# Query features of pair 0 held unturned, and the order around them

## The chip, the cores and the metric

The kernel runs on 1 core of one Trainium2 chip. The time is device microseconds from start to end of one execution. PE is TensorE's matmuls, PEld its weight loads, DVE VectorE, ACT ScalarE, POOL GpSimd, SP SyncE (here it only issues DMAs). "SPq" and "POOLq" are the queues of DMA issues of SP and POOL.

## The reference

A linear attention with sketched quadratic features, then a router that sends each token to one of 8 experts. q, k, v are (4, 4, 1088, 32): batch B, heads H, sequence S, head dimension D. S1 and S2 are (8, 32).

```python
def phi(x):
    a = np.einsum('rd,bhsd->bhsr', S1, x)
    b = np.einsum('rd,bhsd->bhsr', S2, x)
    return np.einsum('bhsi,bhsj->bhsij', a, b).reshape(*x.shape[:-1], r * r)
q_p, k_p = (phi(q), phi(k))                      # 64 features
kv = np.einsum('bhsf,bhsd->bhfd', k_p, v)
z = np.sum(k_p, axis=2)
out = einsum('bhsf,bhfd->bhsd', q_p, kv) / (einsum('bhsf,bhf->bhs', q_p, z)[..., None] + 1e-06)
x = out.transpose(0, 2, 1, 3).reshape(4352, 128)
logits = normed(x) @ normed(expert_emb).T / tau  # (4352, 8)
e = argmax(logits); gate = softmax(logits)[e]
y = gate * (relu(x @ w1[e]) @ w2[e])             # w1 (8, 128, 1024), w2 (8, 1024, 128)
```

## The kernel before

**Tiling.** The four batches are handled as two pairs, m = 0 and 1; the two batches of a pair lie on the two halves of the 128 partitions (u or i). The 1088 positions are 17 tiles (c) of 64 in each batch; GROUPS takes them as four groups of four tiles, the fourth with the single tile 16 (the "rest") beside it. So a group of one pair is 4 x 128 rows by 4 heads.

**Keys, for each group** (`keys`): `tr` turns the rows (L340, four PE transposes, copied to kT by ACT, L342); `ab` sketches them with S1 and S2 (L356; L353 for the rest); `b` copies the second sketch out of PSUM (L362, ACT); `prod` multiplies the two to 64 features (L367, DVE, out kp); `kv` accumulates kp against v and ones in one PSUM bank (L406). After the last group of a pair `total`, `tr_kv`, `kvT` and `kve` (L414 to L433) bring kv, z, and kv times the normalised expert embeddings into kz, the right side of the outputs. So an output matmul gives numerator, denominator and router logits at once.

**Queries, for each group** (`queries`): the same `tr`, `ab`, `b`, `prod` (out qp), then `tr_qp` turns the features (L478, eight transposes into a two-bank PSUM tile, copied by ACT, L481, to qpT), `nd` forms the outputs (L489, 32 matmuls into a two-bank tile), `x` divides and sums the logits (L498 to L505, DVE), `squares` gives the norms (L510 on ACT, L512 on POOL). The queries of pair 0 are ready before its keys are summed; their turned features wait in `held`, which is the second half of the tile of w2 (experts 4 to 7), so that these four experts' w2 are loaded late.

**Router, for each span** of 8 or 9 tiles (`router`): `best` and `pick` (L568 to L580) choose an expert; `place` (L588 to L595) counts on PE, with triangular and one matrices, where each token stands among those of its expert; `split` (L600 to L604), `mark` (L610) and `store` (L615, L616) prepare rows, and `write` (L620) sends them to HBM. Then `count` (L686, L687, out `full`) and `rest` of `plan_early` (L697 to L705), `find`, `digit`, `sums`, `tokens` of `table` (L662 to L679) make the list of tokens of each block of 128. The first 10 blocks (EARLY) come from pair 0 alone, the other 31 (LATE) from what remains of both pairs.

**Experts, for each of 41 blocks:** `fetch` (L736, gather by POOL), `turn` (L742, copied to xTb by DVE, L744), `weights` (L753 and L758 on DVE, L756 on ACT for the first ten: a copy of the chosen expert's w1 and w2 to a tile of its own), `up` (L767, relu L768), `share` (L775, L776), `down` (L782, L784) and the scatter to the output (L787).

**The order** is written out by hand. Each step is a closure put at (tick, rank); the lists are sorted by tick and rank and issued in that order under a manual schedule, so this is the program order of PE, DVE, ACT and POOL. Keys of pair 0 run in ticks 0 to 3 with the queries of pair 0 (K_AT, Q_AT); the outputs of pair 0 in ticks 4 to 7 with the keys of pair 1; the queries of pair 1 in ticks 8, 8, 9 and 10 and its outputs in ticks 8 to 11 (ND_AT); the experts start at tick 10. `put(after, rank, f)` puts f at its tick plus `after`. SP takes its DMAs in program order, and a DMA waits for a queue slot.

**PSUM.** ps_small has two banks (`t`), ps_big two tiles of two banks each (`big`), and `acc` and `ab` have one bank each. In ticks 0 to 3 the sketches of keys and queries of a group lie in the two halves of the one `ab` bank. `ps_big` serves `tr_qp`, `nd` and later `up`.

Of the kernel before, what the change touches and what calls it, by code (L numbers as in the profile page):

```python
# [11 lines left out]
F32 = mybir.dt.float32  # L12
# [7 lines left out]
P = 128  # L20
B, H, S, D = 4, 4, 1088, 32
R = 8
# [35 lines left out]
def kernel(  # L58
# [43 lines left out]
    def load_q(m, c0, c1):  # L102

        for i in range(2):
            r = slice(i * HALF, (i + 1) * HALF)
            at = q.offset + (2 * m + i) * H * S * D + c0 * D
            nc.sync.dma_start(q_sb[m][r, :, c0:c1].rearrange("p h c d -> p h (c d)"),
                              bass.AP(tensor=q.tensor, offset=at, ap=[[NC * D, HALF], [S * D, H], [1, (c1 - c0) * D]]))

# [59 lines left out]

    held = w2_sb[:, E // 2:].rearrange("p e f d -> p e (f d)").rearrange("p e (b n) -> p e b n", b=2)  # L170

# [55 lines left out]
    def iota(shape, pattern, base, mult, name):  # L227
        ti = work.tile(shape, I32, tag="iota", bufs=1, name=name + "_i")
        nc.gpsimd.iota(ti[:], pattern=pattern, base=base, channel_multiplier=mult)
        t = consts.tile(shape, F32, name=name)  # L230
        nc.vector.tensor_copy(t[:], ti[:])
        return t
# [30 lines left out]
    def iotas():  # L263
        li = work.tile([P, P], I32, tag="iota", bufs=1, name="lane_i")
        nc.gpsimd.iota(li[:], pattern=[[1, P]], base=0, channel_multiplier=0)
        nc.vector.tensor_copy(lane, li)
        part = iota([P, 1], [[1, 1]], 0, 1, "part")
        nc.vector.tensor_scalar(before, lane, part[:, 0:1], 1.0 / P, op0=ALU.is_gt, op1=ALU.mult)
        nc.vector.tensor_scalar_mul(lanes, bview(lane, [[1, P], [0, WIDE]]), 1.0 / P)

        nc.vector.tensor_scalar_mul(prefer, lane[:, :E], -1.0 / (2 * E))
        nc.vector.tensor_scalar_mul(base, lane[:, :E], float(KEYS))
        tok_i = work.tile([P, 3, NM * NCP], I32, tag="iota", bufs=1, name="tok_i")
# [69 lines left out]
    def tile_of(n, shape, tag):  # L345
        return work.tile(shape, F32, tag=tag if n > 1 else tag + "1", bufs=2 if n > 1 else 1, name=tag)
# [17 lines left out]

    def features(ab, b, n, tag):
        t = tile_of(n, [P, n, H, R * R], tag)
        nc.vector.tensor_mul(t.rearrange("p j h (i k) -> p (j h) i k", i=R),  # L367
                             ab[:, :, 0].unsqueeze(3).broadcast_to([P, n * H, R, R]),
                             b.unsqueeze(2).broadcast_to([P, n * H, R, R]))
        return t  # L370

    def ab_bank(tick, n):

        if (tick, n) not in ab_ps:
            ab_ps[tick, n] = ps_small()[:, :2 * P] if n == 1 else ps_one("ab")
        return ab_ps[tick, n]

    def keys(m, c0, c1, put):
# [6 lines left out]
        def ab():  # L385
            s["ab"] = sketch(ab_bank(put.tick, n)[:, n * HALF:], s["kT"], n)

# [39 lines left out]
        def kve():  # L427
# [3 lines left out]
            for u in range(2):  # L431
                r = slice(u * HALF, (u + 1) * HALF)
                nc.scalar.copy(kz[m][r, :, :, u, D + 1:], ps[r, :, :, u])  # L433
        put(-1, 52, tr)
        put(0, 50, ab)
        put(0, 51, b)
        put(0, 54, prod)

        first = c0 >= NC - 5 and m == 0
        put(1, 47 if first else 55, kv)  # L440
        if c1 == NC:
            put(1, 47.5 if first else 56, total)
            put(1, 48.5 if first else 60, tr_kv)
            put(1, 48.6 if first else 64, kvT)
            put(1, 53 if first else 82.5, kve)

    xg, ssq, lg, squared = {}, {}, {}, {}

    def queries(m, c0, c1, put, put_nd):
# [15 lines left out]
        def ab():  # L465
            s["ab"] = sketch(ab_bank(put.tick, n)[:, :n * HALF], s["qT"], n)

# [3 lines left out]
        def prod():  # L471
            s["qp"] = features(s["ab"], s["b"], n, "qp")

        def tr_qp():
            ps = ps_big() if n > 1 else ps_small().rearrange("p (b n) -> p b n", b=2)
            for j in range(n):
                for p in range(2):
                    nc.tensor.transpose(ps[:, p, j * P:(j + 1) * P],  # L478
                                        s["qp"][:, j, 2 * p:2 * p + 2].rearrange("p h f -> p (h f)"), ident)
            s["qpT"] = held[:, c0 // 4] if m == 0 and n > 1 else tile_of(n, [P, 2, w], "qpT")  # L480
            nc.scalar.copy(s["qpT"], ps[:, :, :w])  # L481

        def nd():
            ps = ps_big().rearrange("p b (u n) -> p (b u) n", u=2) if n > 1 else ps_small().unsqueeze(1)
            W = 2 * COLS
            for j in range(n):
                for i in range(2):
                    for p in range(2):
# [3 lines left out]
                            kz[m][:, i, p].rearrange("p h d -> p (h d)"), start=True, stop=True)  # L492
            s["hs"] = ps[:, :n, :2 * W].rearrange("p n (h d) -> p n h d", h=H)

        def x():
# [17 lines left out]
        last = c0 >= NC - 5  # L513
        if m == c0 == 0:

            for i, f in enumerate((tr, ab, b, prod)):
                put(0, (51.1, 51.2, 51.3, 54.1)[i], f)
        elif m == 0:
            put(-1, 53, tr)
            put(0, 49, ab)  # L520
            put(0, 50.5, b)
            put(0, 53, prod)
        else:

            behind = c0 == 4
            put(*((0, 53.5) if behind else (-1, 84 if c0 == 8 else 53)), tr)
            put(0, 83 if behind else 49, ab)
            put(0, 83.1 if behind else 50.5, b)
            put(0, 88 if behind else 53, prod)
        if m == 0:  # L530
            put(1, 48 if last else 57, tr_qp)
        else:
            put(*((0, 82) if c0 == 0 else (1, 20)), tr_qp)
        first = m == 1 and c0 == 0
        put_nd(0, 89 if first else 70, nd)
        put_nd(0, 90 if first else 71, x)
        put_nd(*((0, 77) if last else (1, 51.5)), squares)
        if c1 == s1:
            best, pick, place, split, mark, store, write = router(m, s0, s1, g)
            put_nd(0, 80, best)  # L540
            put_nd(0, 81, pick)
            put_nd(1, 64 if m == 0 and c1 == NC else 90, write)

            if c1 < NC:
                put_nd(1, 83, place)
                put_nd(1, 84, split)
                put_nd(1, 85, mark)
                put_nd(1, 86, store)
            elif m == 0:
                put_nd(1, 56, place)  # L550
                put_nd(1, 57, split)
                put_nd(1, 59, mark)
                put_nd(1, 63, store)
            else:
                put_nd(1, 56, place)
                put_nd(1, 57, split)
                put_nd(1, 86, mark)
                put_nd(1, 87, store)

    counts = []  # L560

    def router(m, c0, c1, g):
        n = c1 - c0
# [18 lines left out]
        def place():  # L582
# [3 lines left out]
            hot = oh[m, c0]  # L586
            ps = ps_small()[:, :n * E].rearrange("p (j e) -> p j e", e=E)
            nc.tensor.matmul(ps, before, hot, start=True, stop=False)  # L588
# [4 lines left out]
            counts.append(total[m, c0])  # L593
            s["t"] = work.tile([P, SPAN, E], F32, tag="lt", name="lt")[:, :n]
            nc.vector.tensor_mul(s["t"], ps, hot)  # L595

        def split():

            t0, t1 = m * NCP + c0, m * NCP + c1
            f = work.tile([P, SPAN], F32, tag="mx8", name="mx8")[:, :n]  # L600
            nc.vector.reduce_sum(out=f, in_=s["t"], axis=AX.X)
            nc.vector.tensor_scalar(place_k[:, t0:t1], f, WHOLE, -WHOLE, op0=ALU.add, op1=ALU.add)
# [79 lines left out]
    def tokens_by_expert(rounded, out):  # L682

        ps = ps_small()[:, :E]
        for i, t in enumerate([rounded] + counts):
# [114 lines left out]
    for i, group in enumerate(GROUPS):  # L800
        for tiles in group:
            for m in range(NM):
                keys(m, *tiles, put_at(K_AT[m][i]))
                queries(m, *tiles, put_at(Q_AT[m][i]), put_at(ND_AT[m][i]))
    put_at(0)(0, 90, more_constants)
    put_at(0)(0, 91, iotas)
    put_at(1)(0, 60, norm_emb)
    put_at(2)(0, 56, scale_emb)
    put_at(3)(0, 51, turn_emb)
    put_at(1)(0, 91, lambda: clear(0))  # L810
    put_at(2)(0, 91, lambda: clear(1))
    put_at(3)(0, 57, place_emb)
    put_at(ND_AT[0][-1])(0, 78, lambda: [load_w2(e) for e in range(E // 2, E)])

# [12 lines left out]
    assert first == Q_AT[1][-1]  # L827
    put_at(first)(-1, 73, lambda: turn(0))

# [3 lines left out]
    put = put_at(table1)  # L833
    put(0, 56.5, count)
    put(1, 40, rest)
# [10 lines left out]
    for i in range(NBLK + 1):  # L846
# [6 lines left out]
        if i + 1 < NBLK:  # L853
            put(0, 72, lambda i=i: turn(i + 1))
        if i < NBLK:
# [41 lines left out]
```

## Time and profile before

| what | value |
|---|---|
| median of 3 runs | 252.95 us (252.93 to 253.91) |
| the profiled execution | 255.82 us |
| its span | 253.87 us |
| PE, PEld busy | 223.2 us (88%), 214.1 us (84%) |
| DVE, ACT, POOL busy | 134.2, 118.1, 100.7 us |
| moved by DMA | 24.30 MB, mean 96 GB/s |

A line of the profile has the line number in the kernel, the engine and the operation, then out <- in by the names of tiles. Where a tile was named in a helper, all its users have that line: L340 turns keys and queries both, and L367 is the product of both, told apart by kp and qp. A tile in `held` shows as w_sb, the name of the weights' tile. Times in a timeline are from the span's start. A matmul's record overlaps the next, so for groups the distance of two starts says more than the duration.

Landmarks of the execution before, from its timeline (start, us): first key turn (L340) 6.14; first key and query sketches (L356) 7.47 and 9.84; next pairs of sketches 13.64, 18.80, 24.45; first turn of query features (L478) 17.77; first output (L489) 41.17; DVE full (L687) 61.12; first write of rows (L620) 54.28; the first fetch (L736) 70.03; first matmul of the expert blocks (L767) 77.96; blocks 3, 6 and 7 at 99.10, 112.74 and 116.50; last scatter (L787) 245.32.

### The profile page before, as it was taken

To read this page: it belongs to the slowest core of one execution; us is meant where nothing else is said; L and a number is where in the kernel's file an instruction comes from. 1 tells how busy PE (TensorE), PEld (TensorE's weight loads), DVE (VectorE), ACT (ScalarE), POOL (GpSimd) and SP (SyncE) were. 2 spreads that over 40 slices of the span, in tenths; PEclk is the share of its full clock that TensorE was granted. 3 is DMA by queue.
4 is the path that set the end of the run, shared out by engine and by line. 5 is a ranking of instruction groups with operands and counts; after the bars stand their busy time and mean duration, and the time that the engine had idled before them with its cause. 6 is when DMAs were issued, how large, how long until landed. Compare 5 with 4: busy or idle time off the path is not lost. (4 is left out here: it accounts for less than half of the span.)

```text
span 253.9 us, 6275 instructions
## 1 busy us (share of the span) xinstructions
PE 223.2 (88%) x2455; PEld 214.1 (84%) x2455; DVE 134.2 (53%) x399; ACT 118.1 (47%) x307; POOL 100.7 (40%) x115
## 2 busy tenths in 40 slices
PE   7679498986877989999999999999999999999930
PEld 6467397876766888999999999999999999999930
DVE  4285504899754788773454455455545544554300
ACT  2426225646552776656635444543444354345410
POOL 3001000312081335455654655565556556552330
PEclk9999869999795899999999999999999999999995
DMA  5969999939620021311111111101111111120000
GB/s 142 268 136 348 232 321 343 361 139 271 227 49 12 14 92 46 110 34 40 37 32 34 35 35 43 40 26 35 39 32 44 34 38 32 35 42 25 7 0 0
DMA packets 22174, 24.30 MB, mean 96 GB/s; under 512 B 5306, under 2 KB 18629, under 8 KB 22145
## 3 DMA queue, kind: packets, MB, share of 16 engines
q1 hardware_dynamic: 19520, 18.79, 25.2%
q0 software_dynamic: 2624, 5.11, 8.4%
q8 instruction: 19, 0.31, 0.5%
q14 instruction: 11, 0.08, 0.1%
HBM read 18.09 MB, written 6.26 MB: 96 GB/s over the span
## 5 line engine op out<-in xcount | busy, mean ns | idle before, releaser
L767 PE MATMUL ps_big<-xTb,wb 128*128 128x128 f32 x656 | 82.0, 279 | 3.1 <-DVE xTb L744 2.2
L767 PEld LDWEIGHTS ps_big<-xTb,wb 128*128 128x128 f32 x656 | 78.2, 195 | 3.7 <-DVE xTb L744 2.4
L787 POOL DMA_INDIRECT out_dram<-y,dst_i x41 | 46.6, 1137 | 59.3 <-ACT y L784 47.4
L768 ACT ACTIVATE hT<-ps_big 128x1024 f32<-128x1024 f32 x41 | 42.0, 1024 | 58.5 <-PE ps_big L767 45.3
L736 POOL DMA_INDIRECT xs<-rows,src_i x41 | 40.9, 998 | 21.7 <-DVE xg L500 9.8
L782 PE MATMUL ps_acc<-wb,hT 128*128 128x128 f32 x336 | 41.0, 275 | 0.0
L782 PEld LDWEIGHTS ps_acc<-wb,hT 128*128 128x128 f32 x336 | 39.2, 192 | 0.0
L782 PE MATMUL ps_ab<-wb,hT 128*128 128x128 f32 x320 | 39.0, 275 | 0.0
L782 PEld LDWEIGHTS ps_ab<-wb,hT 128*128 128x128 f32 x320 | 37.4, 192 | 0.0
L753 DVE COPY wb<-w_sb 128x1024 f32 x41 | 28.6, 698 | 13.8 <-issue 12.8
L512 POOL TENSOR_TENSOR xg<-ssq,half_c 128x4 f32<-128x4 f32 (+1 forms) x10 | 9.4, 942 | 46.9 <-ACT sq L510 42.1
L775 DVE TENSOR_SCALAR gate<-gate 128x1 f32<-128x1 f32 x41 | 6.2, 152 | 38.2 <-ACT hT L768 22.9
L758 DVE COPY wb<-w_sb 128x1024 f32 x31 | 21.3, 686 | 0.0
L744 DVE COPY xTb<-ps_t 128x128 f32<-128x128 f32 x41 | 11.9, 290 | 15.8 <-PE ps_t L742 12.7
L367 DVE TENSOR_TENSOR kp<-ps_ab,kb 128x1024 f32<-128x1024 f32 x8 | 9.7, 1211 | 15.0 <-ACT kb L362 9.8
L367 DVE TENSOR_TENSOR qp<-ps_ab,qb 128x1024 f32<-128x1024 f32 x8 | 9.8, 1220 | 9.3 <-ACT kb L362 5.0
L784 ACT ACTIVATE y<-ps_acc,gate 128x128 f32<-128x128 f32 x21 | 7.7, 368 | 12.4 <-PE ps_acc L782 11.9
L784 ACT ACTIVATE y<-ps_ab,gate 128x128 f32<-128x128 f32 x20 | 7.4, 368 | 11.3 <-PE ps_ab L782 10.3
L510 ACT ACTIVATE sq<-xg 128x128 f32<-128x128 f32 x34 | 10.5, 310 | 3.8 <-DVE xg L500 2.9
L742 PE MATMUL ps_t<-ident,xs 128*128 128x128 f32 x41 | 11.4, 278 | 1.0 <-ACT qT L342 0.8
L772 ACT ACTIVATE probs<-xs 128x8 f32<-128x8 f32 x41 | 11.9, 291 | 0.0
L756 ACT COPY wb<-w_sb 128x1024 f32 x10 | 10.4, 1047 | 1.8 <-DMA w_sb<-in_moe_w_dram 1.3
(178 smaller groups left out, 256.8 us busy)
## 6 DMA issues: line engine op xcount, KB each, us to landing
w_sb<-in_moe_w_dram SPq DMA_DIRECT2D x16, 512.0 KB, 8.4
k<-in_k_dram SPq DMA_DIRECT2D x4, 512.0 KB, 5.2
v<-in_v_dram SPq DMA_DIRECT2D x4, 512.0 KB, 7.0
rows<-xg SPq DMA_DIRECT2D x3, 616.5 KB, 3.9
rows<-xg SPq DMA_DIRECT2D x3, 548.0 KB, 2.8
q<-in_q_dram SPq DMA_DIRECT2D x2, 544.0 KB, 7.1
xs<-rows,src_i POOLq DMA_INDIRECT x41
out_dram<-y,dst_i POOLq DMA_INDIRECT x41
```

Source lines behind the costliest of these rows:

```text
L367: nc.vector.tensor_mul(t.rearrange("p j h (i k) -> p (j h) i k", i=R), ab[:, :, 0].unsqueeze(3).broadcast_to([P, n * H, R, R]), b.unsqueez ...
L736: nc.gpsimd.indirect_dma_start(out=xs[i][:], out_offset=None, in_=rows[t][:, :], in_offset=bass.IndirectOffsetOnAxis(ap=src_i[t][:, j:j + ...
L742: nc.tensor.transpose(ps[:, :P], xs[i][:, :DM], ident)
L744: nc.vector.tensor_copy(xT[i], ps[:, :P])
L753: nc.vector.tensor_copy(wb[i][:, 0], w1_sb[:, bass.ds(e, 1)].rearrange("p o f -> p (o f)"))
L758: nc.vector.tensor_copy(wb[i][:, 1], w2)
L767: nc.tensor.matmul(ps[:, u, j * P:(j + 1) * P], w[:, f * P:(f + 1) * P], x, start=True, stop=True)
L768: nc.scalar.activation(hT[i], ps, ACT.Relu)
L772: nc.scalar.activation(p, xs[i][:, DM:DM + E], ACT.Exp, scale=xs[i][:, ROW - 1:], accum_out=gate[i])
L782: nc.tensor.matmul(ps, h[:, f * P:(f + 1) * P], w[:, f], start=f == 0, stop=f == NF - 1)
L784: nc.scalar.activation(y, ps, ACT.Copy, scale=gate.pop(i)[:, 0:1])
L787: nc.gpsimd.indirect_dma_start(out=out[:, :], out_offset=bass.IndirectOffsetOnAxis(ap=dst_i[t][:, j:j + 1], axis=0), in_=y[:], in_offset=N ...
```

## The change

Three things are changed in what is done, and many ranks in the order of it.

- **Loads of q** go by head over all 128 partitions (four DMAs in place of two over 64 partitions each).
- **Pair 0's query features** are written by `prod` into `held` as they are. Their turn (`tr_qp`, now without its copy) and the copy (`qpT`, a step of its own) move from ticks 1 to 4 to pair 1's key ticks: group 0 to tick 4, the others to the tick before their outputs.
- **Banks.** In ticks 0 to 3 `ab_bank` gives the sketches a two-bank tile, one bank for queries and one for keys; from tick 4 on, the halves of `ab` as before. The router's counts go to the unused end of a bank of `nd`'s tile (`spare`) or, for the last span of a pair, to a `table_bank` that also takes the counts by expert. The product of counts and choice moves from `place` to `split`.
- **Order.** The constants and iotas (two buffers now) move from rank 90 of tick 0 to 45; `scale_emb` to rank 45 of tick 2; `turn_emb` and `place_emb` from tick 3 to tick 4; the four late w2 loads from rank 78 to 48 of tick 7, all behind the first write of rows; the second write of rows from rank 64 to 58 of tick 8, with its `store` ahead of the table; `turn(0)` to rank 21 of tick 10, `turn(i + 1)` from rank 72 to 45. In the expert part nothing else is changed.

```diff
     def load_q(m, c0, c1):
-        for i in range(2):
-            r = slice(i * HALF, (i + 1) * HALF)
-            at = q.offset + (2 * m + i) * H * S * D + c0 * D
-            nc.sync.dma_start(q_sb[m][r, :, c0:c1].rearrange("p h c d -> p h (c d)"),
-                              bass.AP(tensor=q.tensor, offset=at, ap=[[NC * D, HALF], [S * D, H], [1, (c1 - c0) * D]]))
+        for h in range(H):
+            nc.sync.dma_start(q_sb[m][:, h, c0:c1].rearrange("p c d -> p (c d)"),
+                              bass.AP(tensor=q.tensor, offset=q.offset + (2 * m * H + h) * S * D + c0 * D,
+                                      ap=[[H * S * D, 2], [NC * D, HALF], [1, (c1 - c0) * D]]))
...
-    def ab_bank(tick, n):
+    def ab_bank(tick, n, u):
         if (tick, n) not in ab_ps:
-            ab_ps[tick, n] = ps_small()[:, :2 * P] if n == 1 else ps_one("ab")
-        return ab_ps[tick, n]
+            ps = ps_small() if n == 1 else ps_big() if tick < n_g else ps_one("ab")
+            ab_ps[tick, n] = ps if n > 1 and tick < n_g else ps[:, :2 * n * HALF].rearrange("p (u n) -> p u n", u=2)
+        return ab_ps[tick, n][:, u, :n * HALF]
...
         def prod():
-            s["qp"] = features(s["ab"], s["b"], n, "qp")
+            t = held[:, c0 // 4].rearrange("p (j h f) -> p j h f", j=4, h=H) if m == 0 and n > 1 else None
+            s["qp"] = features(s["ab"], s["b"], n, "qp", t)
...
-            s["qpT"] = held[:, c0 // 4] if m == 0 and n > 1 else tile_of(n, [P, 2, w], "qpT")
-            nc.scalar.copy(s["qpT"], ps[:, :, :w])
+            s["ps"] = ps[:, :, :w]
+
+        def qpT():
+            s["qpT"] = tile_of(n, [P, 2, w], "qpT")
+            nc.scalar.copy(s["qpT"], s["ps"])
...
+        if m == 0:
+            put(*((0, 51.1) if c0 == 0 else (-1, 53)), tr)
+            put(0, 53.1 if c0 == 0 else 50, ab)
+            put(0, 53.2 if c0 == 0 else 50.5, b)
+            put(0, 54, prod)
+            for i, f in enumerate((tr_qp, qpT)):
+                put_nd(*((0, 47.7 + 0.02 * i) if c0 == 0 else (-1, 57)), f)
+            put_nd(0, 70, nd)
+            put_nd(0, 71.5 if n == 1 else 71, x)
...
-            ps = ps_small()[:, :n * E].rearrange("p (j e) -> p j e", e=E)
+            ps = s["ps"] = bank()[:, :n * E].rearrange("p (j e) -> p j e", e=E)
...
-            s["t"] = work.tile([P, SPAN, E], F32, tag="lt", name="lt")[:, :n]
-            nc.vector.tensor_mul(s["t"], ps, hot)
...
         def split():
+            t = work.tile([P, SPAN, E], F32, tag="lt", name="lt")[:, :n]
+            nc.vector.tensor_mul(t, s["ps"], oh[m, c0])
...
-    put_at(0)(0, 90, more_constants)
-    put_at(0)(0, 91, iotas)
+    put_at(0)(0, 45, more_constants)
+    put_at(0)(0, 46, iotas)
...
-    put_at(2)(0, 56, scale_emb)
-    put_at(3)(0, 51, turn_emb)
+    put_at(2)(0, 45, scale_emb)
+    put_at(4)(0, 47.75, turn_emb)
...
-    put_at(3)(0, 57, place_emb)
-    put_at(ND_AT[0][-1])(0, 78, lambda: [load_w2(e) for e in range(E // 2, E)])
+    put_at(4)(0, 47.9, place_emb)
+    put_at(ND_AT[0][-1])(0, 48, lambda: [load_w2(e) for e in range(E // 2, E)])
...
-    put_at(first)(-1, 73, lambda: turn(0))
+    put_at(first)(0, 21, lambda: turn(0))
...
-            put(0, 72, lambda i=i: turn(i + 1))
+            put(0, 45, lambda i=i: turn(i + 1))
```

More of the change, by code (lines that the diff above doesn't have):

```diff
@@ L168 @@
     w2_sb = consts.tile([P, E, NF, DM], F32, name="w2_sb")
-    held = w2_sb[:, E // 2:].rearrange("p e f d -> p e (f d)").rearrange("p e (b n) -> p e b n", b=2)
+    held = w2_sb[:, E // 2:].rearrange("p e f d -> p e (f d)")
     def load_w2(e):
@@ L227, in iota @@
     def iota(shape, pattern, base, mult, name):
-        ti = work.tile(shape, I32, tag="iota", bufs=1, name=name + "_i")
+        ti = work.tile(shape, I32, tag="iota", bufs=2, name=name + "_i")
         nc.gpsimd.iota(ti[:], pattern=pattern, base=base, channel_multiplier=mult)
@@ L263, in iotas @@
     def iotas():
-        li = work.tile([P, P], I32, tag="iota", bufs=1, name="lane_i")
+        li = work.tile([P, P], I32, tag="iota", bufs=2, name="lane_i")
         nc.gpsimd.iota(li[:], pattern=[[1, P]], base=0, channel_multiplier=0)
@@ L274, in iotas @@
         nc.vector.tensor_scalar_mul(base, lane[:, :E], float(KEYS))
-        tok_i = work.tile([P, 3, NM * NCP], I32, tag="iota", bufs=1, name="tok_i")
+        tok_i = work.tile([P, 3, NM * NCP], I32, tag="iota", bufs=2, name="tok_i")
         nc.gpsimd.iota(tok_i[:, 0].rearrange("p (m c) -> p m c", m=NM), pattern=[[-2 * S, NM], [-1, NCP]], base=NOWHERE,
@@ L363, in second, with features @@
         return b
-    def features(ab, b, n, tag):
-        t = tile_of(n, [P, n, H, R * R], tag)
+    def features(ab, b, n, tag, t=None):
+        if t is None:
+            t = tile_of(n, [P, n, H, R * R], tag)
         nc.vector.tensor_mul(t.rearrange("p j h (i k) -> p (j h) i k", i=R),
@@ L385, in ab @@
         def ab():
-            s["ab"] = sketch(ab_bank(put.tick, n)[:, n * HALF:], s["kT"], n)
+            s["ab"] = sketch(ab_bank(put.tick, n, 1), s["kT"], n)
         def b():
@@ L433, in kve @@
                 nc.scalar.copy(kz[m][r, :, :, u, D + 1:], ps[r, :, :, u])
[L434 to L437, printed above, removed]
+        put(-1, 49.5 if m == 0 and c0 == 4 else 52, tr)
+        ahead = m == 1 and c0 == 0
+        put(0, 47.8 if ahead else 49.8, ab)
+        put(0, 47.9 if ahead else 49.9, b)
+        put(0, 53, prod)
         first = c0 >= NC - 5 and m == 0
@@ L441, in keys @@
         if c1 == NC:
[L442 to L447, printed above, removed]
+            put(1, 47.5 if first else 55.2, total)
+            put(1, 47.705 if first else 55.6, tr_kv)
+            put(1, 47.71 if first else 57.9, kvT)
+            put(1, 53 if first else 58.5, kve)
+    xg, ssq, lg, spare = {}, {}, {}, {}
     def queries(m, c0, c1, put, put_nd):
@@ L465, in ab @@
         def ab():
-            s["ab"] = sketch(ab_bank(put.tick, n)[:, :n * HALF], s["qT"], n)
+            s["ab"] = sketch(ab_bank(put.tick, n, 0), s["qT"], n)
         def b():
@@ L493, in nd @@
             s["hs"] = ps[:, :n, :2 * W].rearrange("p n (h d) -> p n h d", h=H)
+            spare[m, c0] = ps[:, 0, 2 * W:]
         def x():
@@ L513, in queries @@
         last = c0 >= NC - 5
[L514 to L522, printed above, removed]
-        else:
[L525 to L537, printed above, removed]
+        step = c0 // 4
+        if m == 0:
[7 more added lines that the diff above has]
+            put_nd(0, 71.5 if n == 1 else 71, x)
+            put_nd(*((1, 55.3 if n == 1 else 53.6) if last else (1, 53.5)), squares)
+        else:
+            turn_at = ((-1, 53), (0, 53.5), (-1, 59), (-1, 53), (-1, 53))[step]
+            put(*turn_at, tr)
+            put(*((-1, 70.6), (0, 55.8), (0, 49), (0, 22), (0, 22))[step], ab)
+            put(*((-1, 70.7), (0, 58.7), (0, 50.5), (0, 22.1), (0, 22.1))[step], b)
+            put(*((-1, 71.2), (0, 88), (0, 53), (0, 53), (0, 53))[step], prod)
+            put(*((0, 55.5) if c0 == 0 else (1, 20)), tr_qp)
+            put(*((0, 58) if c0 == 0 else (1, 20)), qpT)
+            put_nd(0, 84 if c0 == 0 else 70, nd)
+            put_nd(0, 90 if c0 == 0 else 71, x)
+            put_nd(*((0, 77) if last else (1, 53.5)), squares)
@@ L538, in queries @@
         if c1 == s1:
-            best, pick, place, split, mark, store, write = router(m, s0, s1, g)
+            bank = (lambda: spare[m, c1]) if c1 < NC else (lambda: table_bank[m][:, 0])
+            best, pick, place, split, mark, store, write = router(m, s0, s1, g, bank)
             put_nd(0, 80, best)
             put_nd(0, 81, pick)
-            put_nd(1, 64 if m == 0 and c1 == NC else 90, write)
+            put_nd(1, 58 if m == 0 and c1 == NC else 90, write)
             if c1 < NC:
-                put_nd(1, 83, place)
+                put_nd(1, 70.5, place)
@@ L549, in queries @@
             elif m == 0:
+                put_nd(1, 55.9, lambda: table_bank.append(ps_big()))
                 put_nd(1, 56, place)
                 put_nd(1, 57, split)
+                put_nd(1, 57.2, store)
                 put_nd(1, 59, mark)
-                put_nd(1, 63, store)
             else:
-                put_nd(1, 56, place)
-                put_nd(1, 57, split)
+                put_nd(1, 75, lambda: table_bank.append(ps_big()))
+                put_nd(1, 75.1, place)
+                put_nd(1, 76, split)
                 put_nd(1, 86, mark)
@@ L560, with router @@
     counts = []
-    def router(m, c0, c1, g):
+    table_bank = []
+    def router(m, c0, c1, g, bank):
         n = c1 - c0
@@ L593, in place @@
             counts.append(total[m, c0])
-            s["t"] = work.tile([P, SPAN, E], F32, tag="lt", name="lt")[:, :n]
-            nc.vector.tensor_mul(s["t"], ps, hot)
         def split():
             t0, t1 = m * NCP + c0, m * NCP + c1
+            t = work.tile([P, SPAN, E], F32, tag="lt", name="lt")[:, :n]
+            nc.vector.tensor_mul(t, s["ps"], oh[m, c0])
             f = work.tile([P, SPAN], F32, tag="mx8", name="mx8")[:, :n]
-            nc.vector.reduce_sum(out=f, in_=s["t"], axis=AX.X)
+            nc.vector.reduce_sum(out=f, in_=t, axis=AX.X)
             nc.vector.tensor_scalar(place_k[:, t0:t1], f, WHOLE, -WHOLE, op0=ALU.add, op1=ALU.add)
@@ L682, in tokens_by_expert @@
     def tokens_by_expert(rounded, out):
-        ps = ps_small()[:, :E]
+        ps = table_bank[-1][:, 1, :E]
         for i, t in enumerate([rounded] + counts):
@@ L833 @@
     put = put_at(table1)
-    put(0, 56.5, count)
+    put(0, 75.5, count)
     put(1, 40, rest)
```

## The prediction

> **What bounds the kernel now.** I read the page's table by engine first, then the window table by stage, the waits of PE, the PE timeline of 24 to 42, and the DMA issues. PE is the busiest engine (88%). The chain of waits names only the last store, so the stages have to come from the window table. Its columns are the window and its length, then busy us and (x instructions) of PE, PE's weight loads, DVE, ACT and POOL, then granted clock, DMA share and GB/s.
>
> ```profile
> 6.00:38.00 32.00, 24.05 (x354) 20.84 (x355) 13.32 (x36) 11.55 (x29) 1.50 (x5) 0.89 1.01 260
> 38.00:60.00 22.00, 18.71 (x413) 16.87 (x412) 16.90 (x50) 12.81 (x54) 4.46 (x5) 1.00 0.85 278
> 60.00:78.00 18.00, 12.53 (x162) 10.85 (x157) 13.07 (x41) 9.03 (x22) 6.44 (x7) 0.88 0.48 153
> 78.00:95.00 17.00, 15.65 (x174) 14.54 (x175) 10.83 (x39) 10.23 (x36) 4.39 (x4) 0.83 0.12 44
> ...
> 120.00:140.00 20.00, 20.00 (x182) 20.00 (x181) 10.13 (x28) 9.77 (x22) 10.66 (x10) 1.00 0.14 35
> ```
>
> From 120 on PE is 100% busy at full clock: one expert block each 3.68 us (L767 twice in a row 112.74 to 116.50, then steady). The change touches nothing there, so what the expert blocks start earlier passes one to one to the end. Before it, no engine is full: 6 to 38 has 8 us of PE idle, 60 to 78 has 5.5, and the clock is under 1 in three windows. The waits say where (us in total, times, longest):
>
> ```profile
> PE ps_t L340 <- DVE en_blk L322: 3.5, 1, 3.5
> PE ps_big L767 <- DVE xTb L744: 2.2, 1, 2.2
> PE ps_ab L356 <- DVE qp L367: 1.8, 1, 1.8
> ```
>
> The first is in the timeline (start, us, engine, line; idle before in brackets); the turns behind it cost 1.98 and 1.97 where they cost 1.15 and 1.09 at 22.35 and 23.43. The window table on 3.41 us shows why:
>
> ```profile
> 26.16 0.28 PE L318 MATMUL ps_t<-ident,emb 8*128 8x8 f32 x2
> 29.98 1.09 PE L340 MATMUL ps_t<-ident,k 128*128 128x128 f32 x4 [3.53 <-DVE en_blk L322]
> 31.00 1.98 PE L406 MATMUL ps_acc<-v,kp 128*64 128x64 f32 x32
> 32.91 1.97 PE L478 MATMUL ps_big<-ident,qp 128*128 128x128 f32 x8
> ...
> 41.17 1.04 PE L489 MATMUL ps_big<-kz,w_sb 128*64 128x82 f32 x23 [0.92 <-ACT kz L433]
> ```
> ```profile
> 25.91:29.33 3.42, 0.54 (x10) 0.38 (x7) 2.62 (x4) 0.61 (x4) 0.00 (x0) 1.00 0.97 232
> 29.33:32.74 3.41, 2.76 (x36) 2.46 (x36) 0.59 (x4) 0.59 (x1) 0.00 (x0) 0.50 1.04 240
> 32.74:36.15 3.41, 3.41 (x40) 2.96 (x37) 0.00 (x0) 1.01 (x1) 0.00 (x0) 0.50 1.11 338
> ```
>
> An idle window gives half clock for two windows. It happens again after 63.46:66.87 (2.22 busy) and 73.70:77.11 (1.24 busy); the first expert block at 77.96 takes 3.78 to the next group, 1.95 at full clock.
>
> **Part 1, up to the first output (L489, now 41.17).** What goes: the 3.5 wait, since emb's turn and its placement leave tick 3 for tick 4; the half clock behind it, by starts 0.5 + 0.8 + 0.9 + 0.5 = 2.7; the 1.8 wait of the query sketch for the query product, since keys and queries no longer share a bank; two of pair 0's four turns L478 (0.86 each, 1.7) and the rest's 0.4, now behind the first output; and waits for two turned copies, 0.67 and 0.62. Sum 11.4. What comes: in ticks 0 to 3 both sides lie in one two-bank tile, so the first query sketch waits for the first key product (9.14 to 10.05: 0.9) and the next for the key copy (0.5). That gives 10.0. The constants and iotas now come ahead of the first products on DVE and POOL; DVE is idle until 10.0 in that stretch (0.00 busy in 6 to 10), which covers them; without that cover the first products start up to 1.3 later (one lanes row of 0.82 and smaller ones). A walk instruction by instruction through the order of the new program, with these rows, puts the first output at 30.5, a gain of 10.6. I take the walk; the 0.6 stays in the range. DVE now writes pair 0's query products into the space that held the turned ones, the same 1.21 each: nothing.
>
> **Query loads.** Two loads over 64 partitions become four over 128:
>
> ```profile
> q<-in_q_dram SPq DMA_DIRECT2D x2, 288.0 KB, 9.7
> q<-in_q_dram SPq DMA_DIRECT2D x2, 256.0 KB, 5.4
> ```
>
> While q is in flight the windows move 215 to 241 GB/s, with k and v 342 to 384. The new loads are nearest to k and v in shape (128 partitions), so I take their rate. SP issues two more for each of three loads, 0.6 each; the first 1.2 go ahead of k's second half (lands 13.6, wanted about 13.0 in the walk), which the faster half MB (0.9) nearly repays. Bounds: 0, and +2.5 if they run as q now does (q's second part lands at 16.0, wanted at 13.5).
> The Trainium skill, "DMA: Bandwidth & Descriptors", section Bandwidth, speaks against this part: it asks for 1 MiB or more in a transfer, and has 138 GB/s at 64 KB against 341 at 1 MB; the new loads have 128 to 144 KB. By it (an estimate) half a MB would take 3.8 us instead of the 2.4 that it takes at 215, so 1.4 later, and the total would be near 245.9. No row here has such small loads on the whole width.
>
> **Part 2, pair 1's key ticks, to the expert counts (DVE full L687, now 61.12).** Two turns and the rest's (2.0) and their ACT copies (1.01 each) come in. ACT has 9 us free of 22 there, so the copies are hidden; the turns are not, since DVE (16.90 of 22) and PE alternate. The walk from the first reciprocal to full is 21.9 where it is 18.5 now: 2.0 from the turns, 1.3 from products and outputs that wait on one another through two big banks. Bounds for the latter 0 to 2.6 (twice). Full comes at 53.7: gain 7.4.
> Here a rule of the Trainium skill speaks against the change: "TensorE: Matmul & The Clock Gate", Part 4 (PE-mode transpose), says transposes don't count as busy for the clock in the same way. By that, four turns more in these ticks could bring half clock, 4 x 0.88 = 3.5, total 248. But the turn at 23.43 ran in 1.09 inside windows that all kept 1.00, so the sum goes by the row.
>
> **Part 3, from full to the expert blocks.** The four w2 loads held back (their room holds pair 0's products) now all follow the first row write, and all go ahead of the second; now one load goes ahead and the last lands at 66.1, 11.9 after that write. The write moves from 54.28 to 46.1; one load more is 0.52 MB at 278 GB/s, 1.9: the last lands at 60.0. ACT's first weight copy (L756, waits 1.3 for it now) wants it at about 62: just hidden. The second row write lands at 61 to 62, the first fetch follows, its block is there at 65 and wanted at 67. Between 55.6 and 61.6 PE gets two gaps of 2.9 and 2.0, as DVE works through the table. Up(0), now 77.96, comes at 70.3 (gain 7.7; the pick's six operations, 1.5, now come ahead of the copy of the first turned block, and the 2.2 wait goes). Up(1) waits for the router's product on the shared bank (2.8 idle) and up(4) 2.0 for its copy behind the plan; against that the half clock of up(0) and up(1) goes (1.8 each at most). Up(6), now 112.74, comes at 103.5: gain 9.2. From there nothing differs.
>
> **Sum.** 9.2, less 0.8 for the clock: the gap before up(1) may fall in one window and cost up to 1.7; I take the middle. Gain 8.4. The profiled execution took 255.82 (span 253.87 and 2.0 around it), 2.9 over the median of 252.95; it would go to 247.4, the median to **244.5**.
>
> **Rivals.**
> - Hot throughout: no new gap fills a window and the 1.3 and 2.8 shrink. 240 to 242.5. For it: windows with 2.27 to 2.34 busy (49.81, 56.63) stayed at 1.00. Against: 63.46, with 2.22, did not. Chance 0.16.
> - A smaller gain, 246.5 to 251.7: q loads no faster (+2.5: 247.0); half clock after two of the new gaps (2 x 2.4 as above: about 249); or the change doesn't uncouple what it says, since both sides still share a tile: if each of four ticks waits the 1.8 of now in place of 1.4 in all, +5.8: 250.3. Chance 0.23.
> - No change that a measurement of this kernel can tell (within 0.5%, 1.3 us): 0.05, several of these together.
> - Slower: the four w2 loads, now in one train, compete with row writes and fetches; ACT's first copy L756 stands behind them in ACT's order, and with it the relus of all blocks. It decides from a landing at 62.3; each us later costs one. Above 72, 5.6 us for each load against 1.9 now, the gain is gone; at 74 the time is about 255. For it: SP now waits up to 4.7 for a queue slot among the weight loads. Against: 278 GB/s held through all of 38 to 60. Chance 0.07.
>
> The forecast's own case, 242.5 to 246.5, has 0.49. The range 240.0 to 249.5 takes in it, the hot one and most of the smaller gains, and so the bounds of q, bank waits and clock; about 0.17 stay out. Faster by over 0.5%: 0.49 + 0.16 + 0.23 = 0.88; same 0.05; slower 0.07.
>
> **What the changed profile would show.** Right: no idle of 3.5 at 26, clock 1.00 in 29 to 36, sketches of the first ticks 4 us apart, first L489-like output near 30.5, full near 54, up(3) at 88 to 90 (now 99.1), over 300 GB/s while q loads. Wrong: ACT idle before the first weight copy on w_sb; PEclk at 5 after 55; a query sketch waiting on kp in each tick; the second tick's q turn waiting on DMA. A gain in the first part that is gone at full would mean that the turns cost more than their rows.

## The result, and the profile after

The changed kernel takes **282.0 us** (280.7 to 285.5) where the kernel before takes 253.4 on the same chip: 1.113 times as long, 95% interval 1.105 to 1.120. The forecast was 244.5, range 240.0 to 249.5. A ratio here compares the faster executions of two kernels, a median is over all of them, and some take a few per cent longer at a lower mean clock. The profiled execution took 285.5 with a span of 283.7, 29.9 more than before's span, and all of it arises before the expert blocks run steadily: the seventh block starts at 142.58 in place of 112.74, 29.8 later.

The page after, its slices of 7.1 us (tenths of busy PE, granted clock, DMA, then GB/s):

```profile
PE   8163489985935376996999999999999999999950
...
PEclk9857599997985579797999999999999999999996
DMA  2332691348999510203011111111111111121000
GB/s 89 111 109 79 150 276 48 113 116 244 352 347 272 203 42 0 92 28 119 13 33 37 38 38 34 37 36 42 29 31 38 39 39 34 29 40 28 19 0 1
```

Before, the DMA row began 5969999939620 and the GB/s row 142 268 136 348 232. Now it begins 2332691348999: the inputs trickle in at some 100 GB/s, and the weights, which SP issued from 26.14 on, are issued from 50.63 on. PE's waits say for what:

```profile
PE ps_t L339 <- DMA q<-in_q_dram: 20.5, 8, 4.1
PE ps_big L497 <- ACT qpT L489: 7.7, 1, 7.7
```

And the wait of ACT that stands behind the second line (the first copy of an expert's w2):

```profile
ACT wb L770 <- DMA w_sb<-in_moe_w_dram: 15.8, 1, 15.8
```

PE's timeline shows the first group of queries. The four turns of a group, one for each head, ran within 0.63 before; now each waits 2.5 to 2.8 us for a load of its own, and they start 2.8 to 3.1 us apart:

```profile
8.27 0.30 PE L339 MATMUL ps_t<-ident,q 128*128 128x128 f32 x1 [0.45 <-DMA q<-in_q_dram]
11.10 0.33 PE L339 MATMUL ps_t<-ident,q 128*128 128x128 f32 x1 [2.53 <-DMA q<-in_q_dram]
14.21 0.48 PE L339 MATMUL ps_t<-ident,q 128*128 128x128 f32 x1 [2.78 <-DMA q<-in_q_dram]
17.27 1.33 PE L339 MATMUL ps_t<-ident,q 128*128 128x128 f32 x5 [2.58 <-DMA q<-in_q_dram]
```

128 KB in 3.0 us are 44 GB/s. The window table of the stretch in which SP has issued nothing but pair 1's q (columns as in the prediction: the last two are DMA share and GB/s), first after, then before, where q shares the engines with the first weights:

```profile
47.00:49.00 2.00, 2.00 (x28) 1.83 (x27) 0.69 (x3) 1.43 (x4) 0.00 (x0) 1.00 0.13 51
49.00:51.00 2.00, 1.96 (x38) 1.75 (x38) 0.83 (x1) 1.80 (x4) 0.00 (x0) 1.00 0.13 51
```
```profile
28.00:30.00 2.00, 0.02 (x1) 0.05 (x1) 1.92 (x5) 0.00 (x0) 0.00 (x0) 0.83 0.97 215
```

A share of 0.13 of 16 engines is **two engines**. The packets (the pieces that an engine moves) tell the same: both kernels load pair 1's q in 512 packets of 2176 bytes. Before, a packet takes 156 ns (median) and 11.9 are under way at a time; after, 88 ns, and 2.0 at a time. The packets got faster and the load 3.7 times slower (24.4 us from first to last packet, 6.5 before). The source of the new load has dimensions (2 batches, 64 rows, bytes of a row); in the old one they are (64 rows, 4 heads, bytes), and in k's (128 rows, 4 heads, bytes).

### The profile page after: what moved, and what is told of

It reads as the page before. It is cut to its first block, busy times and chain, and to the rows that moved or that the text cites. A ratio compares the mean times of both kernels' runs of the same rounds, so it can differ in the third digit from the quotient of the medians.

```text
span 283.7 us, 6275 instructions
## 1 busy us (share of the span) xinstructions
PE 230.6 (81%) x2455; PEld 220.6 (78%) x2455; DVE 135.1 (48%) x399; ACT 117.4 (41%) x307; POOL 100.9 (36%) x115
## 5 line engine op out<-in xcount | busy, mean ns | idle before, releaser
L781 PE MATMUL ps_big<-xTb,wb 128*128 128x128 f32 x656 | 84.2, 284 | 7.1 <-DVE gate L789 2.6
L781 PEld LDWEIGHTS ps_big<-xTb,wb 128*128 128x128 f32 x656 | 80.2, 200 | 7.7 <-DVE gate L789 2.8
L801 POOL DMA_INDIRECT out_dram<-y,dst_i x41 | 45.8, 1117 | 61.0 <-ACT y L798 50.8
L750 POOL DMA_INDIRECT xs<-rows,src_i x41 | 42.0, 1024 | 33.0 <-DMA rows<-xg 20.0
L767 DVE COPY wb<-w_sb 128x1024 f32 x41 | 28.4, 696 | 13.7 <-issue 12.7
L339 PE MATMUL ps_t<-ident,q 128*128 128x128 f32 x32 | 8.2, 358 | 21.1 <-DMA q<-in_q_dram 20.5
L339 PEld LDWEIGHTS ps_t<-ident,q 128*128 128x128 f32 x32 | 4.6, 171 | 23.6 <-DMA q<-in_q_dram 21.7
L758 DVE COPY xTb<-ps_t 128x128 f32<-128x128 f32 x41 | 11.9, 291 | 22.4 <-PE ps_t L756 20.4
L497 PE MATMUL ps_big<-kz,qpT 128*64 128x82 f32 x256 | 13.6, 268 | 7.8 <-ACT qpT L489 7.7
L497 PEld LDWEIGHTS ps_big<-kz,qpT 128*64 128x64 f32 x256 | 12.3, 161 | 9.5 <-ACT qpT L489 8.1
L341 ACT COPY qT<-ps_t 128x512 f32<-128x512 f32 (+1 forms) x10 | 5.0, 526 | 24.9 <-PE ps_t L339 24.9
L786 ACT ACTIVATE probs<-xs 128x8 f32<-128x8 f32 x41 | 11.9, 291 | 0.0
```

The costliest lines, as they stand in the source:

```text
L339: nc.tensor.transpose(ps[:, h * P:(h + 1) * P], tiles[:, h].rearrange("p c d -> p (c d)"), ident)
L497: nc.tensor.matmul(ps[i * HALF:(i + 1) * HALF, j, p * W:(p + 1) * W], s["qpT"][:, p, j * P + i * HALF:j * P + (i + 1) * HALF], kz[m][:, i, ...
L750: nc.gpsimd.indirect_dma_start(out=xs[i][:], out_offset=None, in_=rows[t][:, :], in_offset=bass.IndirectOffsetOnAxis(ap=src_i[t][:, j:j + ...
L758: nc.vector.tensor_copy(xT[i], ps[:, :P])
L767: nc.vector.tensor_copy(wb[i][:, 0], w1_sb[:, bass.ds(e, 1)].rearrange("p o f -> p (o f)"))
L781: nc.tensor.matmul(ps[:, u, j * P:(j + 1) * P], w[:, f * P:(f + 1) * P], x, start=True, stop=True)
```

## The experiments

Theory A: an outermost dimension of size 2 puts a load on 2 of 16 DMA engines; the rest of the 29.9 follows, since the weights stand behind q in SP's order. Rival B: loads by head of 128 KB are slow in any shape. Rival D: the new order is slow by itself. "Old loads" below is the changed kernel with `load_q` of before.

**Old loads in the changed kernel.**

```diff
-        for h in range(H): ... ap=[[H * S * D, 2], [NC * D, HALF], [1, (c1 - c0) * D]]
+        for i in range(2): ... ap=[[NC * D, HALF], [S * D, H], [1, (c1 - c0) * D]]
```

> The changed kernel with the q loads of before (two of 64 partitions by batch); everything else of the change stays. Theory A (the outermost dimension of the new q loads has size 2, so each runs on 2 of the 16 DMA engines, 46 GB/s; all else follows from late q, since the weights stand behind q in SP's order): 243 to 249 us, the 247.0 that the prediction gave for q loads no faster; first output at 31 to 34, ACT's wait for the w2 landing under 3 us (15.8 in the changed kernel). Rival D (the new order, above all the four w2 loads in one train behind the row write, makes it slow by itself): ACT still waits over 8 us for w2, 258 us or more.

Median 255.98 (251.96 to 259.07), ratio to before 1.013 (0.996 to 1.031); the profiled execution 252.07, span 250.3. The loss goes, so D falls. But the gain that was forecast isn't there either (the median lies above the 243 to 249 that I expected), and ACT waits 5.0 for w2, not under 3. That is a second error, taken up below.

**New loads in the kernel before** (the same lines, the other way round).

> The kernel before with only the q loads of the change (four by head over 128 partitions). Theory A: slow by itself, 270 to 285 us, with PE waiting some 20 us for q in all and the w loads 20 us later. Rival D: within 3 us of before.

277.65, ratio 1.099 (1.086 to 1.111); PE waits 15.4 for q and 7.6 for a copy behind w2. The loads alone do it.

**The size of the outermost dimension**, 4, 8 and 16 in place of 2, with the same four loads and bytes.

```diff
-  ap=[[H * S * D, 2], [NC * D, HALF], [1, (c1 - c0) * D]]
+  ap=[[8 // w * S * D, w], [NC * D, P // w], [1, (c1 - c0) * D]]     # w = 4, 8
+  ap=[[S * D // 2, 16], [NC * D, 8], [1, (c1 - c0) * D]]             # 16
```

> As the run with size 8, with size 4 (4 pieces of 32 partitions); q again lands in other places, so the output isn't the reference's. Theory A: 4 of 16 engines, share near 0.25, 85 to 100 GB/s, between the others: 252 to 266 us. Rival B: 278 to 286 us.

> The changed kernel with the same four loads of 128 to 272 KB over 128 partitions, but the outermost dimension of the source has size 8 (8 pieces of 16 partitions) in place of 2; every q value is loaded once, but to another place, so the output isn't the reference's. Theory A: 8 of 16 engines, DMA share near 0.5 where q alone is in flight, 150 to 200 GB/s, 245 to 251 us. Rival B (loads by head of 128 KB are slow by themselves, some 3 us each whatever their shape): as slow as the changed kernel, 278 to 286 us.

> The changed kernel with its four loads by head over 128 partitions, the outermost dimension of the source of size 16 (16 pieces of 8 partitions); q lands in other places, so the output isn't the reference's. Theory A: all 16 engines, over 300 GB/s while q alone is in flight, PE waits for q under 0.5 us (1.5 with the old loads), 249 to 255 us: it is what the change would have been with the rate that the prediction gave its q loads. Rival B (loads by head are slow by themselves) is out if the sizes 4 and 8 keep their order, and would make this 278 or more.

Measured, for pair 1's 512 packets (packets under way: the sum of their durations over the time from first to last):

| outermost size | us for the load | under way | median packet | PE waits for q | median us, ratio to before |
|---|---|---|---|---|---|
| 2 (the change) | 24.4 | 2.0 | 88 ns | 20.5 | 282.0, 1.113 (1.105 to 1.120) |
| 4 | 13.6 | 4.0 | 88 ns | 7.5 | 261.6, 1.033 (1.021 to 1.045) |
| 8 | 9.7 | 6.1 | 88 ns | 2.6 | 255.2, 1.002 (0.989 to 1.015) |
| 16 | 6.0 | 11.4 | 88 ns | 0.2 | 254.5, 1.002 (0.998 to 1.007) |
| 64 (old loads) | 6.3 | 12.1 | 150 ns | 1.5 | 256.0, 1.013 (0.996 to 1.031) |

A holds and B falls: number, bytes and width of the loads are the same in the first four rows. The time for size 8 lies over what I expected (245 to 251), as that run inherits the second error. And the last two rows show that the step was not worth taking: with all 16 engines q's wait goes from 1.5 to 0.2 and the first output stays where it was (30.53 and 30.47), since the last turns of q's second group start no earlier (14.25, and 14.30 with the old loads). Nor does q come near the 300 GB/s that I expected of size 16: its 1.11 MB in 6.0 us are 186 GB/s.

**Where the loss arises**: new loads for one pair only (`if m == 1:` or `if m == 0:` around them).

> The changed kernel, with pair 0's q loaded as before and only pair 1's q by head. It splits the cost of the slow loads: late queries of pair 0 in the first 40 us against the queue behind pair 1's q, where all weights stand. Theory A: the four loads take 24 us and push the weights 8 to 12 us; PE waits for q of pair 1 (4 to 6 us near 45) and ACT for w2 10 us or more: 258 to 266 us. If only the first ticks mattered: 253 to 256, as with the old loads.

> The reverse: pair 0's q by head, pair 1's as before. Theory A: PE waits some 16 us for q in the first 40 us, all later stages move with it, weights too: 264 to 274 us. The excesses of this run and of the other over the run with old loads should add up to about the 26 us of the whole. If only the weights' delay mattered: under 260.

Pair 1 only (three executions, 263.2 to 270.2): profiled 267.47, span 265.7, 15.4 over the span with old loads; PE waits 7.7 for q, ACT 15.0 ahead of its first w2 copy (put down to a row write in the same queue), and PE 7.3 for the copy behind it. Pair 0 only (269.65, 274.7, and one of 344.0 with a mean clock of 0.64, left unexplained): profiled 269.65, span 267.9, 17.6 over; PE waits 15.7 for q, ACT 5.3 for w2, as with old loads. Together 33.0, and the changed kernel has 33.4. By the fastest execution of each the excesses over old loads (251.96) are 11.2 and 17.7, together 28.9, and the changed kernel has 28.8: the sum holds either way, the share of each is less sure. So pair 0's loads cost by the waits of the first ticks, pair 1's by their own wait and by the weights behind them in the queue, each a large part. Both medians (267.5 and 274.7) lie just above what I expected.

**Why old loads gain nothing: the clock.** With old loads the first output comes at 30.47, as forecast, 10.7 earlier than before; the seventh expert block comes at 109.14, only 3.6 earlier. Its windows, laid on the moments at which the granted clock changes (first number after POOL):

```profile
53.50:56.91 3.41, 1.42 (x33) 1.25 (x32) 3.14 (x17) 0.77 (x3) 0.00 (x0) 1.00 1.00 265
56.91:60.33 3.42, 1.19 (x17) 1.09 (x17) 2.07 (x6) 1.08 (x2) 0.00 (x0) 0.50 1.07 402
...
67.15:70.57 3.42, 1.08 (x20) 0.94 (x20) 2.71 (x10) 1.27 (x3) 1.91 (x2) 1.00 0.18 41
70.57:73.98 3.41, 2.76 (x13) 2.77 (x14) 0.56 (x3) 0.00 (x0) 0.00 (x0) 0.50 0.02 5
...
94.46:97.87 3.41, 1.11 (x10) 0.92 (x9) 3.17 (x14) 2.49 (x5) 1.40 (x2) 1.00 0.55 202
97.87:101.28 3.41, 3.09 (x14) 3.09 (x15) 2.41 (x6) 0.00 (x0) 1.37 (x2) 0.50 0.17 46
```

Three windows with 1.1 to 1.4 us of PE work, each followed by half clock: 17.1 us in all, as much as before had, but on other work.

How long such a stretch lasts depends on what PE has to do in it. The prediction read two windows of half clock from the first stretch of before; the second one there was a single window long, and that window was full of work:

```profile
63.46:66.87 3.41, 2.22 (x35) 1.94 (x34) 2.31 (x9) 1.96 (x6) 0.00 (x0) 1.00 0.33 113
66.87:70.29 3.42, 3.42 (x36) 3.09 (x31) 2.86 (x8) 1.26 (x2) 0.26 (x1) 0.50 0.79 311
```

Laid on these windows, from the first clock record to the tail, all fourteen profiles agree. A window at full clock with at most 1.54 us of PE work was always followed by half clock, one with more than 2.25 us never; between the two both happened (1.75 us at 77.39 with old loads stayed at full). A window at half clock was followed by full clock when it held 3.0 us or more, and by another at half when it held 2.8 or less.

With old loads, the first expert block stands in the second of the three stretches, behind a copy that waits for the router's pick on DVE:

```profile
71.22 3.78 PE L782 MATMUL ps_big<-xTb,wb 128*128 128x128 f32 x16 [2.98 <-DVE xTb L759]
```

To test it, matmuls of zeros that nothing uses were put into PE's five gaps, and the router's pick behind the first turned block's copy on DVE (`fill(bank, n)` issues n of these matmuls):

```diff
+    put_at(ND_AT[0][-1] + 1)(0, 84.5, lambda: fill("acc", 9))
+    put_at(ND_AT[0][-1] + 1)(0, 86.5, lambda: fill("acc", 7))
+    for i, tag, n in ((0, "acc", 12), (1, "acc", 8), (4, "ab", 10)):
+        put_at(first + i)(0, 29.5, lambda tag=tag, n=n: fill(tag, n))
...
-            put_nd(0, 80, best)
-            put_nd(0, 81, pick)
+            late_pick = m == 1 and c1 < NC
+            put_nd(*((1, 22.5) if late_pick else (0, 80)), best)
+            put_nd(*((1, 22.6) if late_pick else (0, 81)), pick)
```

> The changed kernel with the q loads of before, and matmuls of zeros put into PE's five gaps between 55 and 98 us (9, 7, 12, 8, 10 of them, 0.22 us each at full clock), to a bank that is free there. They compute nothing that is used. Theory C (what the new order gains is given back by half clock after its new gaps: 6.8 us of it from 59, 6.8 from 72, 3.4 from 99): clock 1.00 from 55 to 110, first expert block 1.95 in place of 3.78, blocks from the seventh on 4 to 6 us earlier than without the fill, 246 to 250 us. Rival E (DVE sets the pace there, and the clock costs nothing that DVE doesn't): within 1.5 us of the kernel without the fill.

> The changed kernel with the q loads of before, and the router's best and pick of pair 1's first span put behind the copy of the first turned block on DVE (six operations, 1.5 us, which stand ahead of it in the change). If DVE's order costs that: the first block starts 1.5 us earlier and so do the ones after it. If the start is set by the clock's windows: 0 to 1 us, either sign.

> Both: q loads of before, matmuls of zeros in the five gaps, pick behind the first block's copy. Theory C with the DVE order's 1.5: 244 to 249 us, the lowest of these and 5 us or more under before. Rival E: within 1.5 us of the kernel with old q loads alone.

Fill: 249.1, ratio 0.981 (0.976 to 0.987). Late pick: 251.7, its executions too far apart (246.6 to 254.5) for an interval. Both: **247.6, ratio 0.978 (0.972 to 0.985)**, the fastest here. The execution of both ran at full clock up to its tail, and its blocks are where the walk had put them, though the walk had neither the fill nor the late pick:

```profile
70.11 1.95 PE L783 MATMUL ps_big<-xTb,wb 128*128 128x128 f32 x16
77.34 2.02 PE L783 MATMUL ps_big<-xTb,wb 128*128 128x128 f32 x16 [0.47 <-DVE lt L615]
...
94.07 2.05 PE L783 MATMUL ps_big<-xTb,wb 128*128 128x128 f32 x16 [0.33 <-DVE xTb L760]
97.86 1.95 PE L783 MATMUL ps_big<-xTb,wb 128*128 128x128 f32 x16
103.57 2.03 PE L783 MATMUL ps_big<-xTb,wb 128*128 128x128 f32 x16
```

From first output to seventh block: 78.7 with old loads, 76.1 with the late pick, 73.2 with the fill, 73.3 with both; the walk had 73.0. So theory C holds: the clock takes 5.5. The late pick brings 2.6 without the fill: 1.5 less wait ahead of the first block (1.45, not 2.98) and a shorter time at half clock (13.7, not 17.1). Beside the fill it brings nothing: the first block's copy then starts at 66.63, but the fill ahead of the block (2.9 us) holds it until 70.11.

**The control: fill in the kernel before**, 14, 5, 4 and 9 matmuls in its own four gaps.

> The kernel before with matmuls of zeros in its own four gaps (14 behind the turn of the embeddings, 5 ahead of the token sums, 4 and 9 ahead of the first expert block), so that both kernels can be compared at full clock. Half clock costs it 2.7 us at 30, about 1.6 at 67 and 3 at 77. If the new order is worth what the walk says (8 or 9 us without clock losses), it stays 2 to 5 us over the changed kernel with old loads, fill and late pick (247.6): 249 to 252. If the fill is the whole gain: 247 to 248.

253.3, ratio 0.990 (0.983 to 0.997); I expected 249 to 252. The fill works in its place (no half clock behind it; from the turn of the embeddings to the first output 12.25 us, 15.0 without), but in the profiled execution all of the first stage had come 3.3 later (that turn at 29.43, not 26.16). Its early matmuls ran at about half speed: the first four turns took 1.12 us, where they took 0.66 in before, and the first clock record is at 20.04, not at 5.43. So this profile isn't one at full clock throughout, as the control was meant to be. By the two ratios the new order with the late pick is worth some 1.2%, 3 us, where both have the fill; the intervals overlap (0.972 to 0.985 and 0.983 to 0.997), so this size is an estimate. With the 3.3 taken off, the control's seventh block would come at 108.1, 4.6 behind the 103.57 of the new order; that is an estimate too.

**The w2 train.** With fill and late pick, each late w2 load is issued as soon as its quarter of the held features is turned:

```diff
-    put_at(ND_AT[0][-1])(0, 48, lambda: [load_w2(e) for e in range(E // 2, E)])
+    for e, tick in zip(range(E // 2, E), (5, 5, 6, 7)):
+        put_at(tick)(0, 40, lambda e=e: load_w2(e))
```

> The changed kernel with old q loads, fill and late pick, and each of the four late w2 loads issued as soon as its quarter of the held features is turned, so that three of them go ahead of the first row write. If the train of w2 behind the row write costs (the prediction's slower rival, in a kernel without slow loads): ACT's wait for w2, 6.3 us, falls by 3 or more and the time by 1 to 3 us. If the wait is hidden: time within 1 us, either sign.

ACT's wait falls from 6.3 to 2.2, and the stretch from first output to seventh block stays at 73.3, so the wait is hidden. The median, 251.3 (ratio 0.982, 0.963 to 1.001), is 3.7 above that of fill and late pick, which I expected of neither case; in the profile the loss lies ahead of the first output (35.26, not 30.23).

## Why the prediction was wrong, step by step

Landmarks (us from the span's start):

| landmark | before | forecast | after | old loads | old loads, fill, pick |
|---|---|---|---|---|---|
| first output | 41.17 | 30.5 | 49.95 | 30.47 | 30.23 |
| full | 61.12 | 53.7 | 76.88 | 52.87 | 52.62 |
| ACT's first w2 copy | 66.14 | 60 to 62 | 94.09 | 59.25 | 60.38 |
| up(0) | 77.96 | 70.3 | 104.30 | 71.22 | 70.11 |
| up(3) | 99.10 | 88 to 90 | 124.99 | 91.62 | 87.56 |
| up(6) | 112.74 | 103.5 | 142.58 | 109.14 | 103.57 |

- **Query loads: the step that failed.** "The new loads are nearest to k and v in shape (128 partitions), so I take their rate", with "+2.5 if they run as q now does" as the far bound. I compared the loads by their width and not by the order of dimensions in their source; no row of before has a load with 2 outermost, so the row of q was no bound. The runs show 2 engines and 46 GB/s in its place, and a price of 33.4 in place of 0 to 2.5. The other bound was off as well: q at its old rate cost nothing (30.47, and 30.53 with size 16).
- The Trainium skill has it. "DMA: Bandwidth & Descriptors", section Rules for kernel authors (the row on using all 16 engines), says that an outermost dimension of fewer than 16 confines the whole DMA to at most that many engines. The runs with 2, 4, 8 and 16 agree: 2.0, 4.0, 6.1 and 11.4 packets under way. From the same page, section Bandwidth, I weighed the rule on small transfers, whose figures are for loads issued from GpSimd; the run with 16 does not bear it out for these, issued from SP: four loads of 272 KB took 6.0 us where two old ones of 544 KB took 6.3.
- **Part 1** was right: 3.5 of wait and the half clock behind it went, and the sketches follow as in the walk (30.47 against 30.5). Of the two sums the walk was the better. Part of the match is luck: the walk has q at the rate of k and v, 342 to 384 GB/s, where pair 1's q moved at 186 with size 16 and 177 with the old loads, and it came out all the same because the first output is the same with either.
- **Part 2** was right within 1: full at 52.87 against 53.7. The four moved turns brought no half clock: with old loads PE stays at 1.00 from 6 to 56. The rule of the Trainium skill that was weighed against it ("TensorE: Matmul & The Clock Gate", Part 4) doesn't show here: the window of before from 8.85, with 2.30 us of PE work of which 0.97 is no transpose, was followed by full clock, and the one with old loads from 53.50, with 1.42 of which 1.38 is none, by half. The row was the better guide.
- **Part 3** was right on the w2 landing (59.25 against 60.0, and hidden, as the early-w2 run shows), though ACT was there 5.0 earlier and not at 62, and on the waits of up(1) and up(4) (2.3 and 2.6 with old loads; 2.8 and 2.0 forecast).
- **Sum, the term of the clock** was mis-sized: 0.8, bound 1.7, in place of 5.5. I had named the gaps (2.9 and 2.0 at 55.6 to 61.6, the one at 75) and priced only the third, though before's own windows with 1.24 and 2.22 busy were each followed by half clock. The rival of a smaller gain had the mechanism, half clock after two of the new gaps, at 2.4 each, a price for which no row stands in the prediction; PEclk at 5 after 55, its sign of being wrong, is what the profile with old loads shows. With the right size the sum would have been a gain of 3.7, and the repeated runs with old loads (ratio 0.996 to 1.031) don't even confirm that.
- **The slower rival** named the mechanism that took a large part of the loss, ACT's first w2 copy behind a late landing: 94.09. By its price of 1 us for each us above 62.3 that gives 276 (244.5 + 31.8), near the 282.0 that were measured. But the cause was not the train that it named; it was q ahead of all weights in SP's order.

**What stays open.** Executions of one kernel lie 3 to 8 us apart, with the new order and good loads (252 to 259 with old loads) and before (250.1 to 258.2 beside them). In the profiles of the new order the first output is at 30.2 to 30.7 in four, at 31.9 with pair 1's new loads only, at 34.0 in the one with the fill and at 35.3 in the one with early w2; in the last two PE waits 3.0 and 4.1 for k and q where it waits 1.8 with old loads alone, and half clock follows in these early ticks. What makes those first loads land later in some executions wasn't settled, and it hides gains of 1%. A fill cut to the gap behind the late pick wasn't tried.

## What to carry to other kernels

Compare loads by their access pattern's outermost dimension, not by bytes or partitions: with 2 there a load used two engines, and everything behind it in its queue paid too. When a wait is removed, lay the new gaps of PE on the windows of its clock and price each; here a gain that left windows of 3.41 us with 1.4 us of work or less was given back at half clock. And where no row of the profile has the shape of a new transfer, its cost has no upper bound from the profile: say so in the range.

## What the runs showed that I had not expected

A packet of 2176 bytes takes 88 ns (median) in the loads by head over 128 partitions, with 2, 4, 8 or 16 outermost, and 150 to 164 ns in the loads by batch over 64 (before, old loads, and old loads with fill and pick). What of their shape does it wasn't separated, and the faster packets bought nothing here: 6.0 us on 16 engines against 6.3. SP also spends longer issuing the confined loads: 5.98 us for the first four against 1.37 for the two of before. And matmuls that compute nothing, 46 of them, took the kernel with old loads from 1.013 to 0.981 of the time of before: they stand in idle time of PE and end the half clock behind it.
